# A planned attention-and-expert kernel: one shared stretch of 64-wide products, first sums of values in another bank, constant rows kept, first high parts in place, VectorE charged more in the order

## The chip, the cores and the metric

One core of a Trainium2 chip runs the whole program. TensorE multiplies, VectorE and ScalarE read its banks in PSUM (the accumulator memory, eight banks of 512 float32 columns), GpSimd does little, and SyncE only issues transfers. The metric is the device time of one execution in microseconds. Times of instructions come from one profiled execution.

## What is computed

Decayed causal attention over 8 batches and 8 heads of 576 positions with 64 columns, followed by a gated feed-forward layer over the 4608 positions:

```python
scores = scale * np.matmul(q, k.transpose(0, 1, 3, 2))
cum = np.cumsum(np.log(np.clip(f, 0.0001, 1.0)), axis=-1)
scores = np.where(causal, -1e9, scores + cum[:, :, :, None] - cum[:, :, None, :])
attn = softmax(scores)                       # with 1e-9 added to the sum
x = (attn @ v)                               # heads side by side: 4608 x 512
h = x @ w_in                                 # 512 -> 2048
g = h * np.tanh(log1p(np.exp(h)))
out = g @ w_out                              # 2048 -> 512
```

## The kernel before

The attention is worked in 32 groups (`g`), two heads each, four groups to a batch. `prep(g)` scales a group's q and k and splits each into a high and a low float16 part in the tile `hl`, of which there is one (`NHL = 1`). Transfers carry the parts into two tiles that TensorE reads: `ST1` (three buffers; rows 0 to 63 the high parts of q and k, rows 64 to 69 the cumulative decay in three float16 parts with rows of constants against them, row 70 a maximum) and `ST2` (the low parts). The decay rows of group 0 come straight from `cum3`; those of the other groups, constants included, from `cumd` in device memory, one transfer of seven rows for a group.

Groups 0 to 5 are done in an early form: `max_items` finds row maxima by a first set of scores, `fin` sends them as the row `mr` into row 70, `st_items` makes the scores again with keys in the partitions and `pv_items` multiplies float32 weights with values. Groups 6 to 31 are done in another: `new_st_items` makes scores with queries in the partitions (pieces x, y, z, w), VectorE masks them and takes the minimum, ScalarE the exponent, ScalarE and VectorE split the result, and a transfer transposes it; `new_pv_items` multiplies with the values, head 0 in `one(0)`, head 1 in `one(1)`. The last 64 queries of the two heads share a tile: their scores are piece w (`w_`), with the scores of the last 64 keys (V) in a bank of their own, and their value products are `tail`. Both issue products whose output has 64 partitions, two of which run side by side; `beside` keeps such a stretch together. Products with 128 output partitions stand before and after each stretch.

The feed-forward layer is worked in nine chunks of 512 positions (`m1_items`, `m2_items`). Its weights (`wall`, 32 blocks) are loaded as 64-bit words, converted and split into two float16 parts by VectorE and ScalarE while attention goes on; its products are the 3456 "wall" products of 128x512. The first four groups (one batch) must be through before the first of them.

The order of all this is not written by hand. Every instruction is recorded by `choose` and put out by `emit` (so that nearly all carry one line, L307). `schedule` runs a planner that lists instructions engine by engine: `forward` takes, on each engine, the ready instruction of lowest rank; where an instruction may run on more than one engine (`choose` with several ways) `sooner` compares the ends it plans, with a charge `PEN` for each engine. `floors` keep an instruction from being planned before a time. Where the planner expects TensorE to wait early on, it puts in filler products (`b<-idh`, 128x128) into bank 7 until the first wall product. On the chip each engine takes its list strictly in order and waits at semaphores.

From group 6 on attention's banks are two (0 and 1), taken in turn by `bank`: nine uses for a group. Banks 2 and 3 take the first layer's products, 4 to 7 the second's. SyncE's queue has eight lanes; a transfer waits until the one eight before it has landed.

Of the kernel before, what the change touches and what calls it, by code (L numbers as in the profile page):

```python
# [13 lines left out]
F16 = mybir.dt.float16  # L14
# [51 lines left out]
NGH = 5  # L66
SPD = 0
# [6 lines left out]
PEN = dict(vector=0, scalar=0, gpsimd=4000)  # L74
# [72 lines left out]
class Program:  # L147
# [24 lines left out]
    def choose(self, *ways):  # L172

        r, w, opts = [], [], []
        for way in ways:
            total, port = 0.0, False
            for nth, (eng, method, a, kw) in enumerate(way):
# [5 lines left out]
                if eng == "tensor":  # L183

                    w.append((w[0][0] + "/pe", 0, 1, 0, 1))
# [411 lines left out]
def attn_moe(ctx: ExitStack, tc: tile.TileContext, qk, v, f, w_in, w_out, out):  # L597
# [62 lines left out]
    cumd = dp.tile([7, BH, 2, S], F16, name="cumd")  # L660
# [7 lines left out]

    def decay():
        _, on, cm, r1 = tmp  # L670
        cst = ST1[2][0:BH].rearrange("p j t s -> p (j t) s")
        x = ST1[0]
        nc.vector.memset(x[64:71, :, 0], -1.0)
        nc.gpsimd.memset(x[64:71, :, 1], -MSC)
        nc.gpsimd.memset(x[64:67, :, 1], 1.0)
        for j, c in enumerate((1.0, -1.0, 0.0, -MSC)):
            nc.gpsimd.memset(cst[:, j], c)
        nc.floor = 12500.0
        nc.sync.dma_start(
            out=cumd[0:3, :, 1].rearrange("r h s -> h r s"),  # L680
            in_=cst[:, 0:1].to_broadcast([BH, 3, S]))
        nc.sync.dma_start(
            out=cumd[3:6, :, 0].rearrange("r h s -> h r s"),
            in_=cst[:, 1:2].to_broadcast([BH, 3, S]))
        nc.sync.dma_start(out=cumd[6], in_=cst[:, 2:4])
        nc.floor = 0.0
# [62 lines left out]
    def all_sum(cols, name, least=2.0**-60):  # L749
# [4 lines left out]
        sum_rows(a, m, bank(name))  # L754
# [133 lines left out]
    def amax_v(b):  # L888
# [3 lines left out]
        vam[b] = all_sum(cols, f"va{b}")  # L892
# [30 lines left out]
    st = {g: {} for g in range(B * NP)}  # L923
# [22 lines left out]
    def prep(g):  # L946
# [15 lines left out]
        hl = sp.tile([P, 4, S], F16, name=f"hl{g}", tag="hl", bufs=NHL)  # L962
        for j, (hi, lo) in enumerate(((1, 3), (2, 0))):
# [5 lines left out]
        if g:  # L969
            nc.sync.dma_start(  # L970
                out=ST1[i][64:71].rearrange("r j t s -> r (j t s)"),
                in_=cumd[:, h0 : h0 + 2].rearrange("r j t s -> r (j t s)"))
# [290 lines left out]
    def new_pv_items(g):  # L1263
# [29 lines left out]
        def one(j):  # L1293
# [4 lines left out]
            if j:  # L1298
                tail(o[:, 4])
# [393 lines left out]
```

## Time and profile before

| | us |
|---|---|
| median of 3 runs | 1038.97 (1038.34 to 1054.77) |
| the profiled execution, its own time | 1042.22 |
| its span, first to last instruction | 1040.4 |
| TensorE busy in it | 1005.0 (97%) |
| VectorE busy | 708.0 (68%) |
| ScalarE busy | 671.8 (65%) |

A matmul's busy time in the profile reaches from its issue to its end, 0.38 us for 512 columns, and overlaps the next; what TensorE takes for one is the distance between starts. A busy share near 100% therefore says that it had no gap longer than that overlap. The waits "<-" name what ended an idle time.

### The profile page before, as it was taken

How to read it: one execution, taken by the hardware profiler on the slowest of the kernel's cores; microseconds unless marked ns; L12 is line 12 of the kernel's file. 1: busy time of each engine (PE TensorE's matmuls, PEld its weight loads, DVE VectorE, ACT ScalarE, POOL GpSimd, SP SyncE). 2: the span in 40 equal slices, each digit the busy share in tenths (PEclk: the TensorE clock that was granted, in tenths of full speed). 3: DMA queues.
4: the chain of work that ended last, by engine and by line, in shares of the span. 5: the costliest groups of instructions: out<-in, count | busy, mean ns of one | idle time of the engine just before them, and what ended most of it. 6: DMA issues, size and time to landing. Idle time of an engine off the chain costs nothing.

```text
span 1040.4 us, 20074 instructions
## 1 busy us (share of the span) xinstructions
PE 1005.0 (97%) x7428; PEld 534.3 (51%) x7428; DVE 708.0 (68%) x1972; ACT 671.8 (65%) x1214; POOL 12.8 (1%) x60
## 2 busy tenths in 40 slices
PE   4899999999999999999999999999999999999998
PEld 3788554444545555545455555444555554444443
DVE  7799999988767777677867876778776663121211
ACT  4557898877777887777768786778777672112111
POOL 3000000000000000000000000000000000000000
PEclk9899999999999999999999999999999999999999
DMA  7899967799766876787758766676666432000001
GB/s 210 254 261 242 225 186 190 180 209 194 142 133 138 185 148 139 143 172 145 150 129 163 170 149 137 152 158 121 129 136 132 77 66 65 1 1 31 11 1 41
DMA packets 252805, 143.47 MB, mean 138 GB/s; under 512 B 220349, under 2 KB 221129, under 8 KB 252706
## 3 DMA queue, kind: packets, MB, share of 16 engines
q1 hardware_dynamic: 252706, 142.18, 61.1%
q8 instruction: 58, 0.95, 0.4%
q14 instruction: 41, 0.34, 0.1%
HBM read 48.33 MB, written 12.57 MB: 59 GB/s over the span
## 4 chain that ended last, share of the span: by engine, by line
PE 62%; DVE 17%; ACT 9%; DMA 5%; issue 5%; SPq 1%; ACTq 0%; DVEq 0%
PE b L307 61%; DVE b L307 3%; DVE wall L307 3%; DMA st<-hl 3%; DVE hb L307 2%; ACT st L307 2%; ACT L307 2%; ACT hb L307 2%; DVE hl L307 1%; DVE gl L307 1%; SPq L307 1%; DMA pt<-hb 1%; ACT junk L307 1%; ACT me L307 1%; DVE vv L307 1%
## 5 line engine op out<-in xcount | busy, mean ns | idle before, releaser
L307 PEld LDWEIGHTS <-wall 128*128 128x128 f16 x3456 | 332.1, 98 | 382.1 <-issue 7.6
L307 PE MATMUL b<-xa,wall 128*128 128x512 f16 x1728 | 408.4, 382 | 0.0
L307 PE MATMUL b<-gh,wall 128*128 128x512 f16 x1152 | 360.5, 379 | 0.2
L307 PE MATMUL b<-gl,wall 128*128 128x512 f16 x576 | 218.3, 379 | 0.0
L307 ACT ACTIVATE st<-b,mn 128x512 f32<-128x512 f32 (+1 forms) x260 | 125.6, 525 | 117.8 <-DVE mn L307 86.5
L307 ACT ACTIVATE me<-b,cinv 128x512 f32<-128x512 f32 x144 | 93.2, 685 | 124.2 <-PE b L307 123.5
L307 PE MATMUL b<-st 70*128 70x256 f16 (+14 forms) x948 | 141.4, 287 | 24.1 <-DVE qt L307 14.8
L307 DVE TENSOR_SCALAR gh<-me,gsc 128x512 f16<-128x512 f32 x121 | 57.7, 484 | 140.3 <-ACT me L307 138.6
L307 ACT ACT_TABLE_LOAD x112 | 143.7, 1283 | 9.2 <-DVE mn L307 6.5
L307 DVE TENSOR_TENSOR hb<-st,hb 128x512 f16<-128x512 f32 x156 | 106.8, 689 | 59.6 <-ACT hb L307 59.0
L307 PEld LDWEIGHTS <-st 70*128 70x128 f16 (+5 forms) x948 | 74.2, 103 | 83.7 <-issue 28.6
L307 PE MATMUL b<-vv,pt 128*128 128x65 f16 (+5 forms) x2520 | 114.2, 205 | 2.7 <-ACT st L307 1.4
L307 DVE CUSTOM_DVE_ANT_0 b<-b,mskw 128x512 f32<-128x512 f32 (+1 forms) x208 | 101.7, 501 | 21.5 <-PE b L307 15.0
L307 ACT ACTIVATE hb<-st 128x512 f16<-128x512 f32 x156 | 97.0, 628 | 9.5 <-DMA pt<-hb 8.5
L307 DVE SCALAR_TENSOR_TENSOR gl<-me,gsc,gh 128x512 f16<-128x512 f32 x144 | 103.1, 745 | 0.0
L307 PEld LDWEIGHTS <-pt 128*128 128x128 f16 (+1 forms) x2184 | 65.6, 101 | 17.0 <-issue 5.0
L307 DVE SCALAR_TENSOR_TENSOR hl<-qk,qt,hl 128x576 f16<-128x576 f32 x64 | 50.6, 808 | 0.2 <-ACT hl L307 0.2
L307 ACT ACTIVATE junk<-qk 128x576 bf16<-128x576 f32 x64 | 43.5, 680 | 4.8 <-DMA qk<-in_qk_dram 4.0
L307 DVE SCALAR_TENSOR_TENSOR wall<-wall 128x512 int32<-128x512 int32 x64 | 42.8, 684 | 0.1
L307 PEld LDWEIGHTS b<-vv,pt 128*128 128x128 f32 (+1 forms) x336 | 39.1, 186 | 4.7 <-issue 1.4
L307 DVE DVE_READ_ACCUMULATOR2_ANT mn<- 128x1 f32 x260 | 36.8, 142 | 0.0
L307 ACT ACTIVATE ot<-b,cols 128x512 f32<-128x512 f32 x36 | 24.3, 688 | 16.1 <-PE b L307 11.6
(105 smaller groups left out, 630.8 us busy)
## 6 DMA issues: line engine op xcount, KB each, us to landing
st<-hl SPq DMA_DIRECT2D x192, 144.0 KB
qk<-in_qk_dram SPq DMA_DIRECT2D x32, 576.0 KB
v<-in_v_dram SPq DMA_DIRECT2D x32, 288.0 KB
out_dram<-ot SPq DMA_DIRECT2D x36, 256.0 KB
wall<-in_w_in_dram SPq DMA_DIRECT2D x16, 512.0 KB
wall<-in_w_out_dram SPq DMA_DIRECT2D x16, 512.0 KB
pt<-hb SPq DMA_TRANSPOSE x156
part<-ot SPq DMA_DIRECT2D x8, 256.0 KB
```

The source lines that it names most:

```text
L307: r = getattr(real[eng], method)(*a, **kw)
```

## The change

Five edits. One: from group 10 on, `w_` of group g is no longer an item of its own; `one(1)` of group g-1 calls it, and its 64-wide products and those of `tail` of group g-1 are one `beside` stretch. The scores V take the last 128 columns of the bank that holds `one(1)`'s output, so a group takes eight banks' turns. Two: `all_sum` of the first two batches' values uses bank 7 (`RB`) instead of a turn. Three: `cumd` holds the three decay parts alone; the constants are set once in each `ST1` buffer, and a group's decay comes in two transfers of three rows (`move_cum`). Four: for groups 0 and 1 (`ND = 2`) the high parts for `ST1` are also written straight into it by ScalarE or VectorE, four instructions of 64x576 in place of two transfers. Five: `PEN` of VectorE is 400, and two floors are 12500 (one was 13000, one zero).

```diff
-PEN = dict(vector=0, scalar=0, gpsimd=4000)
+PEN = dict(vector=400, scalar=0, gpsimd=4000)
...
+    def move_cum(x, h):
+        for t, r in enumerate((64, 67)):
+            if h:
+                nc.sync.dma_start(out=x[r : r + 3, :, t], in_=cumd[h : h + 2].rearrange("h r s -> r h s"))
+            else:
+                for j in range(2):
+                    nc.sync.dma_start(out=x[r : r + 3, j, t], in_=cum3[j : j + 1])
...
-        for j in range(2):
-            for t, r in enumerate((64, 67)):
-                nc.sync.dma_start(out=x[r : r + 3, j, t], in_=c[j : j + 1])
-        nc.sync.dma_start(out=cumd[0:3, :, 0].rearrange("r h s -> h r s"), in_=c)
-        nc.sync.dma_start(out=cumd[3:6, :, 1].rearrange("r h s -> h r s"), in_=c)
+        move_cum(ST1[0], 0)
+        nc.sync.dma_start(out=cumd, in_=cum3)
...
-        vam[b] = all_sum(cols, f"va{b}")
+        vam[b] = all_sum(cols, bank(f"va{b}") if b > 1 else psum(RB))
...
+        for j in range(2 * (g < ND)):
+            for h in range(2):
+                r = slice(h * D, (h + 1) * D)
+                nc.choose(*(scaled(ST1[i][0:D, h, j], x[r, j], t[r, j : j + 1], e) for e in SV))
...
-        for j in range(2):
+        for j in range(2 * (g >= ND)):
             nc.sync.dma_start(out=ST1[i][0:D, j], in_=hl[j * D : (j + 1) * D, 1:3])
...
             ps, pv = bank(f"sw_{g}"), bank(f"sv_{g}")
+            if with_tail:
+                st[g - 1]["o1"], pv = pv, pv[:, CH - P : CH]
...
+            if with_tail:
+                every = every[4:] + every[0:4] + st[g - 1]["tail"](st[g - 1]["o1"][:, 4 * (D + 1) : 5 * (D + 1)])
             beside(*every)
...
+            if j and 9 <= g < NG - 1:
+                st[g + 1]["w"]()
+                o = s["o1"]
...
-            a0(lambda: held(13000.0, lambda: load_v(0, VTA)))
+            a0(lambda: held(12500.0, lambda: load_v(0, VTA)))
```

What the planner makes of it stands in the lists of the engines. TensorE's list has the same products, in another order, with 166 fillers where it had 252. Late in the steady part of the program, before the change, one group's tail products (`64x65` into bank 0, two weights of the group's tile `pt`) and the next group's piece w (`64x512` into bank 1, `64x128` into bank 0) stand apart, with expert products around each:

```order
L307 MATMUL b0_0_125<-vv_0_128,pt_6_148 64x65
L307 LDWEIGHTS wall_69
L307 MATMUL b3_0_119<-xa1_87,wall_69 128x512
...
L307 MATMUL b2_0_118<-xa1_87,wall_69 128x512
L307 LDWEIGHTS st1_1_82
...
L307 MATMUL b1_0_116<-st2_1_85 64x512
L307 LDWEIGHTS st1_1_82
L307 MATMUL b0_0_125<-st1_1_82 64x128
...
L307 MATMUL b0_0_125<-st2_1_85 64x128
L307 LDWEIGHTS wall_69
L307 MATMUL b2_0_118<-xa1_87,wall_69 128x512
```

The same place of the change, where bank 0 holds the scores V and the output of `one(1)`:

```order
L309 MATMUL b2_0_118<-xa1_87,wall_69 128x512
L309 LDWEIGHTS st1_0_81
L309 MATMUL b0_0_125<-st1_0_81 64x128
...
L309 MATMUL b0_0_125<-st2_0_84 64x128
L309 LDWEIGHTS st1_0_81
L309 MATMUL b1_0_117<-st1_0_81 64x512
...
L309 MATMUL b1_0_117<-st2_0_84 64x512
L309 LDWEIGHTS pt_3_136
L309 MATMUL b0_0_125<-vv_1_141,pt_3_136 64x65
...
L309 MATMUL b0_0_125<-vv_1_141,tv_1_186 128x65
```

V, w and the tail now follow each other without a 128-wide product between, and the head's other value products come right behind, into the bank that still holds V.

On SyncE near the start, from the first products' rows on, before the change (`st1_0`, `st1_1`, `st1_2` are the buffers of `ST1`; "x4" is four alike):

```order
L307 DMA st2_0_84<-hl_0_109 64x1152 x3
L307 DMA cumd_89<-cum3_90 64x3x576 x2
L307 DMA st2_0_84<-hl_0_109 64x1152
L307 DMA v32_0_110<-in_v_dram 128x576
...
L307 DMA st1_1_82<-cumd_89 7x2304
L307 DMA qk32_0_103<-in_qk_dram 128x1152
L307 DMA st1_1_82<-hl_0_109 64x1152 x2
L307 DMA st2_1_85<-hl_0_109 64x1152 x4
L307 DMA wall_69<-in_w_in_dram 128x1024 x2
L307 DMA st1_2_83<-cumd_89 7x2304
L307 DMA qk32_1_104<-in_qk_dram 128x1152
L307 DMA st1_0_81<-mr_0_127 1x4x128 x2
```

and of the change:

```order
L309 DMA v32_2_112<-in_v_dram 128x576
L309 DMA st1_0_81<-cum3_90 3x1x576 x4
L309 DMA cumd_89<-cum3_90 64x1728
L309 DMA st2_0_84<-hl_0_109 64x1152 x4
L309 DMA v32_3_113<-in_v_dram 128x576
L309 DMA st1_1_82<-cumd_89 3x2x576 x2
L309 DMA qk32_0_103<-in_qk_dram 128x1152
L309 DMA wall_69<-in_w_in_dram 128x1024 x2
L309 DMA st1_2_83<-cumd_89 3x2x576
L309 DMA st1_0_81<-mr_0_127 1x4x128 x2
L309 DMA st1_0_81<-mr_0_127 1x2x64
L309 DMA st2_1_85<-hl_0_109 64x1152 x4
```

Three value loads now stand ahead of the decay rows; the three transfers of constants and those of the high parts of groups 0 and 1 are gone, and group 0's `mr` rows come ahead of group 1's low parts.

On VectorE, where group 1's high parts are made, before the change (`qt_1` is the group's scale, `mx_0` group 0's maxima):

```order
L307 RECIPROCAL qt_1_123<-qt_1_123 128x1
L307 TENSOR_REDUCE mx_0_117<-b2_0_118 128x4
...
L307 TENSOR_REDUCE mx_0_117<-b5_0_121 128x1 x2
L307 TENSOR_SCALAR hl_0_109<-qk32_1_104,qt_1_123 128x576
L307 TENSOR_REDUCE mx_0_117<-b6_0_124 128x2
```

and of the change:

```order
L309 TENSOR_TENSOR mx_0_116<-mx_0_116 128x9
...
L309 RECIPROCAL qt_1_122<-qt_1_122 128x1
L309 TENSOR_SCALAR st1_1_82<-qk32_1_104,qt_1_122 64x576
L309 COPY mr_0_127<-b1_0_117 9x128
L309 TENSOR_SCALAR hl_0_109<-qk32_1_104,qt_1_122 128x576
L309 TENSOR_SCALAR st1_1_82<-qk32_1_104,qt_1_122 64x576 x2
```

Group 0's maxima are finished first, and the casts then go straight into `st1_1`.

## Rows read from the trace of the kernel before

**Rows 1.** The page, busy time of each engine (share of the span), instructions

```profile
PE 1005.0 (97%) x7428; PEld 534.3 (51%) x7428; DVE 708.0 (68%) x1972; ACT 671.8 (65%) x1214; POOL 12.8 (1%) x60
```

**Rows 2.** Windows: length, then PE, PEld, DVE, ACT, POOL busy, PEclk, DMA share, GB/s

```profile
42.00:101.00 59.00, 59.00 (x608) 49.16 (x609) 52.84 (x160) 40.57 (x92) 0.75 (x5) 1.00 0.92 241
101.00:165.00 64.00, 59.56 (x360) 35.27 (x358) 59.57 (x169) 54.40 (x106) 0.28 (x2) 0.95 0.77 204
165.00:240.00 75.00, 71.58 (x522) 35.23 (x521) 69.87 (x214) 61.95 (x115) 0.28 (x2) 0.98 0.88 196
240.00:865.00 625.00, 619.61 (x4868) 316.50 (x4867) 457.41 (x1293) 467.29 (x823) 3.33 (x22) 1.00 0.68 141
```

**Rows 3.** Windows at half clock, the same columns

```profile
153.60:160.40 6.80, 6.80 (x23) 3.28 (x23) 5.54 (x15) 5.79 (x14) 0.14 (x1) 0.50 0.52 146
228.70:232.10 3.40, 3.40 (x10) 1.18 (x8) 2.23 (x9) 2.52 (x7) 0.00 (x0) 0.51 0.59 139
```

**Rows 4.** Timeline of TensorE at the start: start, length, what, count, idle before

```profile
14.83 0.27 PE L307 MATMUL b<-st 70*128 70x128 f16 x1 [14.83 <-DVE qt L307]
...
30.82 0.27 PE L307 MATMUL b<-st 70*128 70x128 f16 x1 [0.28 <-DMA st<-hl]
...
36.27 5.49 PE L304 MATMUL b<-idh 128*128 128x128 f16 x85
41.59 0.53 PE L307 MATMUL b<-st 71*128 71x512 f16 x2
...
45.56 0.39 PE L307 MATMUL b<-vv,pt 128*128 128x65 f32 x2
...
101.23 0.81 PE L307 MATMUL b<-xa,wall 128*128 128x512 f16 x3
```

**Rows 5.** Timeline of SyncE's issues at the start

```profile
9.32 2.95 SPq L307 DMA_DIRECT2D st<-cum  x4
...
23.59 4.71 SPq L307 DMA_DIRECT2D st<-hl  x6
...
34.34 2.09 SPq L307 DMA_DIRECT2D st<-mr  x3
```

**Rows 6.** Timeline of VectorE between 15 and 24 us

```profile
15.02 0.16 DVE L307 RECIPROCAL qt<-qt 128x1 f32<-128x1 f32 x1
15.88 3.35 DVE L307 TENSOR_REDUCE mx<-b 128x4 f32<-128x512 f32 x7 [0.70 <-PE b L307]
...
23.04 0.52 DVE L307 TENSOR_SCALAR hl<-qk,qt 128x576 f16<-128x576 f32 x1 [1.50 <-issue]
```

**Rows 7.** Timeline of TensorE around one tail and one piece w

```profile
513.69 0.25 PE L307 MATMUL b<-vv,tv 128*128 128x65 f16 x3
513.87 0.57 PE L307 MATMUL b<-vv,pt 128*64 128x65 f16 x24
514.37 1.69 PE L307 MATMUL b<-xa,wall 128*128 128x512 f16 x7
...
523.77 0.74 PE L307 MATMUL b<-st 70*64 70x512 f16 x8
524.45 1.90 PE L307 MATMUL b<-xa,wall 128*128 128x512 f16 x8
```

**Rows 8.** Groups by form on VectorE and ScalarE: count, busy us, mean ns, idle before

```profile
L307 DVE TENSOR_SCALAR gh<-me,gsc 128x512 f16<-128x512 f32 x121 | 57.7, 484 | 140.3 <-ACT me L307 138.6
L307 DVE TENSOR_SCALAR hl<-qk,qt 128x576 f16<-128x576 f32 x40 | 20.4, 514 | 15.3 <-DMA st<-hl 11.4 <-issue 3.7
...
L307 ACT ACTIVATE hl<-qk,qt 128x576 f16<-128x576 f32 x24 | 18.3, 772 | 9.3 <-DVE qt L307 6.3 <-DMA st<-hl 2.8
L307 ACT ACTIVATE gh<-me,gsc 128x512 f16<-128x512 f32 x23 | 16.1, 717 | 0.0
```

**Rows 9.** Waits of TensorE between 101 and 240 us: total, times, longest

```profile
PE b L307 <- ACT st L307: 3.2, 4, 1.8
PE b L307 <- ACT pt L307: 2.0, 3, 1.4
```

More of the change, by code (lines that the diff above doesn't have):

```diff
@@ L66 @@
 NGH = 5
+ND = 2
 SPD = 0
@@ L183, in choose @@
                 if eng == "tensor":
-                    w.append((w[0][0] + "/pe", 0, 1, 0, 1))
+                    out = kw["out"] if "out" in kw else a[0]
+                    w.append((out.tensor.name + "/pe", 0, 1, 0, 1))
                 port |= self.shared(eng, method, aps)
@@ L659, in attn_moe @@
     BH = B * H
-    cumd = dp.tile([7, BH, 2, S], F16, name="cumd")
+    cumd = dp.tile([BH, 3, S], F16, name="cumd")
     cum3 = cp.tile([BH, 3, S], F16, name="cum3")
@@ L667, in attn_moe @@
     ft = tmp[0]
+    def move_cum(x, h):
[5 more added lines that the diff above has]
+                    nc.sync.dma_start(out=x[r : r + 3, j, t], in_=cum3[j : j + 1])
     def decay():
         _, on, cm, r1 = tmp
[L671 to L686, printed above, removed]
+        for i, x in enumerate(ST1):
+            (nc.gpsimd if i else nc.vector).memset(x[64:71, :, 0], -1.0)
+            nc.gpsimd.memset(x[64:71, :, 1], -MSC)
+            nc.gpsimd.memset(x[64:67, :, 1], 1.0)
         nc.vector.memset(on, 1.0)
@@ L747, in sum_rows, with all_sum @@
         nc.vector.tensor_copy(out=out, in_=ps)
-    def all_sum(cols, name, least=2.0**-60):
+    def all_sum(cols, ps, least=2.0**-60):
         m = sp.tile([P, 1], F32, name="am_m", tag="am_m", bufs=3)
@@ L753, in all_sum @@
         a = col()
-        sum_rows(a, m, bank(name))
+        sum_rows(a, m, ps)
         return a
@@ L920, in scale_chunk3 @@
             out=cosc[c], in0=cix[c], scalar=1.0 / GSH, in1=top[:, i : i + 1], op0=ALU.mult, op1=ALU.mult)
-    st = {g: {} for g in range(B * NP)}
+    NG = B * NP
+    st = {g: {} for g in range(NG)}
     banks = list(range(NA))
@@ L969, in prep @@
         if g:
-            nc.sync.dma_start(
-                out=ST1[i][64:71].rearrange("r j t s -> r (j t s)"),
-                in_=cumd[:, h0 : h0 + 2].rearrange("r j t s -> r (j t s)"))
-        for j in range(2):
+            move_cum(ST1[i], h0)
+        for j in range(2 * (g >= ND)):
             nc.sync.dma_start(out=ST1[i][0:D, j], in_=hl[j * D : (j + 1) * D, 1:3])
@@ L1168, in new_st_items @@
     def new_st_items(g):
+        with_tail = 9 < g < NG
         i = place1(g)
@@ L1257, in w_ @@
             turn(e, "W")
+        if with_tail:
+            s["w"] = w_
+            return [
+                (begin, 0), (lambda: x_(0), 440), (lambda: y_(0), 440), (z_, 440),
+                (lambda: x_(1), 440), (lambda: y_(1), 440)]
         return [
@@ L1280, in tail @@
         def tail(o):
-            for a in products(o, s["V"], 0, slice(0, P), s["vh"][:, 8], s["vl"][:, 8], True, False):
-                mm(*a)
             every = []
@@ L1288, in tail @@
                     both.append(products(
-                        o[r], s["W"], kt, r, s["vh"][:, 2 * kt + j], s["vl"][:, 2 * kt + j], False, kt == 3))
+                        o[r], s["W"], kt, r, s["vh"][:, 2 * kt + j], s["vl"][:, 2 * kt + j], kt == 0, False))
                 every += [a for x in zip(*both) for a in x]
-            beside(*every)
+            return every
+        s["tail"] = tail
         def one(j):
             n = 4 + j
-            o = bank(f"o{j}_{g}", (P, n, D + 1))
+            if j and 9 <= g < NG - 1:
+                st[g + 1]["w"]()
+                o = s["o1"]
+            else:
+                o = bank(f"o{j}_{g}")
+            o = o[:, 0 : n * (D + 1)].rearrange("p (n d) -> p n d", d=D + 1)
+            if j:
+                if not 9 <= g < NG - 1:
+                    beside(*tail(o[:, 4]))
+                for a in products(
+                        o[:, 4], s["V"], 0, slice(0, P), s["vh"][:, 8], s["vl"][:, 8], False, True):
+                    mm(*a)
             for qt in range(4):
                 blocks(o[:, qt], j, qt)
-            if j:
-                tail(o[:, 4])
             rr = sp.tile([P, 5], F32, name=f"rr{g}_{j}", tag="rr", bufs=4)[:, 0:n]
@@ L1484, in ranked @@
         return g
-    NG = B * NP
     nc.sync.dma_start(out=ft, in_=f)
@@ L1602, in attn_moe @@
             r = KS0 + i * KSS
-            wq.append(ranked([r, 0, 0.1], lambda i=i: convert_weights(i)))
+            wq.append(ranked([r, 0, 0.1], lambda i=i: held(12500.0, lambda: convert_weights(i))))
             wq += [ranked([r + 5, 0, 0.1], lambda k=k: load_weights(k)) for k in behind.get(i, [])]
```

## Prediction

> **What bounds the kernel now.** I read the page's busy times first: TensorE 1005.0 of 1040.4 us, VectorE 68%, ScalarE 65% [rows 1]. So TensorE's own stream sets the time, and a change is worth what it takes out of that stream or out of its gaps. Then the windows, to see where other engines hold it up. Between 240 and 865 us TensorE lacks 625.0 - 619.6 = 5.4 us, and VectorE and ScalarE are busy 73% and 75%: there only TensorE's own stream counts. Between 101 and 240 us it lacks 4.44 + 3.42 = 7.9 us while VectorE is busy 93% in both windows and ScalarE 85% and 83% [rows 2]: here the weights are converted beside attention and all three engines are near their limit. Between 42 and 101 us TensorE is busy throughout (59.0 of 59.0) and VectorE 90% [rows 2]. Before 42 us TensorE mostly waits or runs fillers: its first product is at 14.83, group 1's first at 30.82, the first product of the second scores at 41.59, behind 85 fillers of 5.49 / 85 = 0.065 us, and the first value product at 45.56 [rows 4]. Nothing after 865 us holds attention, so the change has no part there.
>
> **Part one, the shared stretch.** A stretch of 64-wide products costs more than its columns. A 512-column product takes 0.217 us from start to start ((1.90 - 0.38) / 7 for the eight at 524.45, with 0.38 the length of one; the seven at 514.37 give (1.69 - 0.38) / 6 = 0.218), so 65 columns take 0.028 and 128 take 0.054. Tail: three wide products from 513.69 end their slots at 513.77, and the first 64-wide one starts at 513.87: 0.10 us to go in. Its 24 in pairs are 12 x 0.028 = 0.34 us, to 514.21; the next wide one starts at 514.37: 0.16 to come out. Piece w: 523.77 to 524.45 is 0.68 us; its eight in pairs, two of 512 columns and two of 128, are 0.54, so 0.14 to come out, and again some 0.10 to go in [rows 7]. Each stretch thus pays about 0.24 us. One stretch in place of two saves one such payment in groups 10 to 31, 22 times: 22 x 0.24 = **5.3 us**, all of it in TensorE's own stream. The two stretches bound it by 22 x 0.24 and 22 x 0.26, 5.3 and 5.7; what a new wait takes from it is a rival below.
>
> **Part two, the start.** What goes: three transfers of constants on SyncE's queue and, for groups 0 and 1, the transfers of high parts. Those held group 1 up twice. Its scale was ready at 15.02 + 0.16 = 15.2 us, but the cast had to wait for the one tile `hl` (idle 1.50 before 23.04) [rows 6], the transfers were issued from 23.59 [rows 5], and the product came at 30.82 [rows 4]. In the change VectorE first finishes group 0's maxima: two casts more, then reductions from about 16.5 us (15.88 before) for the seven of 3.35 us and two or three more at some 0.5 [rows 6], to about 21.5; eight small instructions at 0.16 to 22.8; then casts at 0.5 into `st1_1`, whose form the trace does not have; the nearest rows are 0.514 for the larger cast on VectorE and 0.772 on ScalarE [rows 8], and I take 0.5. Four make 2.0. Group 1's products then start at about 25 us, 6 earlier. Group 0's `mr` rows are copied at about 23.3; three issues are 2.09 us; the decay rows, issued until 9.32 + 2.95 = 12.27, were in use by 14.83, so such a transfer lands within 2.6 us [rows 4, 5]: 28.0. With group 1's maxima and 41 fillers between, the second scores start at 28 to 31, I take 30: 11.6 us before the old 41.59.
>
> Not all of that stays. The new list has 11 + 8 + 23 + 9 = 51 fillers between those scores and the first value product, where there was none: 51 x 0.065 = 3.3 us. And VectorE, whose list there holds two converted weights, group 2's low parts and group 1's maxima ahead of the values' scale, has some 13 us of work from 26.6 on (25 instructions at 0.15 to 0.2, eleven of about 0.7, two reductions of 0.55): the first value product can start at 38 to 41. I take 39.5, that is 6.0 earlier than 45.56. From there to 101 us TensorE was never idle, so the lead is carried; 35 later fillers against 23 take back 12 x 0.065 = 0.8. Lead at the first wall product: **5.2 us**. Bounds: 10.8 (the scores' lead less 0.8) if VectorE's list is shorter than I think, 2 if the three value loads ahead of the decay rows delay group 0. The two transfers for one in `move_cum` cost 31 more issues of 0.3 to 0.7 us; SyncE is not waited for in the steady part, and at the start the three constants' transfers and four others are gone, so nothing.
>
> **Part three, VectorE's charge.** The lists show up to about 225 us (the seventeenth low part of the gated layer) five casts `gh`, five `hl`, two of the weights and one of x gone from VectorE to ScalarE. At 0.484 and 0.514 [rows 8] and 0.45 for the others that is 2.4 + 2.6 + 1.4 = 6.4 us off VectorE, and at 0.717 and 0.772 [rows 8] 3.6 + 3.9 + 2.1 = 9.6 onto ScalarE. After 240 us both have a quarter of their time free, so the rest of the moves is worth nothing. In 101 to 240 us TensorE loses 7.9 us to gaps, and 6.8 x 0.5 + 3.4 x 0.5 = 5.1 us more to two stretches at 1.2 GHz [rows 3], each behind a gap: 13 in all. A VectorE that is less full and starts earlier takes some of it; but of the gaps 3.2 + 2.0 us end with ScalarE [rows 9], which goes from 116.4 busy us of 139 to 126 (91%). Bounds: minus 10 (nearly all of it) and plus 3 (ScalarE's gaps grow by their half). I take **minus 5**, between them and nearer to the gain, because the earlier conversions also bring the wall products that fill such gaps.
>
> **The clock.** Of the fillers' loss I count nothing. On the rows TensorE fell twice after a wait to a granted clock of 0.50, the 1.2 GHz level, in 153.6 to 160.4 and 228.7 to 232.1 us, and 6.8 us at that level cost 3.4 [rows 3]. The Trainium skill, "TensorE: Matmul & The Clock Gate", section "HAM oscillation — how this bites in real kernels", says that idle gaps drop the clock and that the next products then run at half rate; by it, 86 fillers fewer are 86 chances more to start the second scores slow. One more stretch of the length seen would make the sum 3.4 us worse; that lies in the range.
>
> **Sum.** 5.3 + 5.2 + 5 = 15.5. Against the profiled execution's own time, 1042.2, this gives 1026.7; that execution lay 3.2 above the median of the runs, 1038.97, so for the median **1023.5**.
>
> **Rivals.**
> *The whole lead is kept.* TensorE is full from 42 to 101 us, so if the first values come with the scores the lead there is 10.8, the crowded part gives 9, the stretches 5.3: 25, time 1014. For it: group 1's hold-up disappears entirely. Against it: 51 new fillers say that the planner too sees a gap there. Chance 0.22.
>
> *ScalarE or the loads take it back.* ScalarE at 91% between 101 and 240 us ends TensorE's gaps more often, or the decay rows wait behind 0.86 MB of values so that the start gains nothing. Either leaves the 5.3 of the stretches: about 1034. For it: ScalarE already ends 5.2 of 7.9 us of gaps [rows 9]. Against it: the maxima of group 1 no longer pass through a transfer. Chance 0.27.
>
> *Slower: the shared bank is held.* V's scores sit in the bank that the tail, the three V products and 30 further value products write right behind. If VectorE may read V only after them, w's exponent comes 0.50 (513.87 to 514.37 [rows 7]) + 33 x 0.028 = 1.4 us later, and w's bank and this one come free as much later for the next pieces. With two banks in turn nothing else of attention can go on; only expert products cover it, 15 in the list there, 15 x 0.217 = 3.3 us, against 1.4 us of writing plus about 3 us of reading by VectorE and ScalarE. If the cover fails in full, 22 x 1.4 = 31 us are added: 1054. It decides from 15.5 / 22 = 0.70 us for a group. The Trainium skill, "PSUM — Partial Sum Buffer", section "PSUM bank collisions raise a hardware error", demands that no two engines touch a bank's quadrant at once, which is the reason such an order must hold; no row here shows an overlap. Against it: the whole steady part has only 5.4 us of gaps [rows 2], so cover planned this way mostly holds. Chance 0.05.
>
> **How the numbers follow.** The forecast, 1023.5 with a range of its own from 1018 to 1030, has 0.46; 1014 has 0.22, 1034 0.27, 1054 0.05. Two per cent, about what a measurement of this kernel can tell from no change, is 20.8 us: faster means below 1018.2, slower above 1059.7. Faster: 0.20 from the first rival and 0.05 from the edge of the forecast, 0.25. Slower: 0.02, the far side of the bank. Within 2%: 0.73. The range from 1012 to 1034 holds nearly all of the forecast (0.45), most of the lead's case (0.19) and a good half of the third (0.16): 0.80.
>
> **What would show each step.** Stretches: 26 pairs before; after, 22 stretches of 32 products with one payment of about 0.24 us. Start: group 1's first product near 25 us, second scores near 30, first value product near 39.5, first wall product (101.23 before [rows 4]) near 96. Crowded part: TensorE's gaps in the 139 us behind the first wall product under 5 us, half-clock stretches gone or fewer. Bank: gaps of TensorE in the steady part, 5.4 now, not above 10. The prediction is wrong if the first wall product is not earlier by 2 us, or if those steady gaps more than double.

## The result, and the profile after

The changed kernel took 1030.03 us in the median, against 1042.31 for the kernel before in the same comparison. The ratio is 0.989 with a 95% interval of 0.986 to 0.992: some 11 us faster, inside the 2% band. The profiled execution took 1030.97 us, 11.25 less than the one of before. Executions of one and the same kernel differ by TensorE's mean granted clock (the changed kernel: 1024.79 us at 1.000, 1029.08 at 0.998, 1030.97 at 0.997 and 1042.58 at 0.984), and the ratio leaves out the slow ones (1042.58 here, 1054.77 of the kernel before), which the two medians hold.

The page of the changed kernel, busy time of each engine, answers [rows 1]:

```profile
PE 990.4 (96%) x7342; PEld 527.2 (51%) x7342; DVE 701.7 (68%) x1958; ACT 693.2 (67%) x1236; POOL 17.5 (2%) x62
```

Windows of the changed kernel (columns as in [rows 2]; the first wall product is at 96.43 now):

```profile
38.00:96.40 58.40, 58.24 (x593) 49.00 (x593) 53.23 (x155) 37.02 (x81) 0.46 (x4) 0.97 0.92 235
96.40:165.00 68.60, 64.67 (x407) 38.44 (x404) 67.41 (x205) 65.56 (x131) 0.50 (x2) 1.00 0.72 207
165.00:240.00 75.00, 68.21 (x531) 34.11 (x531) 61.26 (x180) 59.06 (x110) 0.28 (x2) 0.98 0.89 187
240.00:865.00 625.00, 619.26 (x4874) 317.15 (x4873) 458.07 (x1300) 473.14 (x820) 3.05 (x22) 1.00 0.68 140
```

TensorE still lacks 5.7 us of the 625 in the steady part (5.4 before). From 96.4 to 240 us it lacks 3.9 + 6.8 = 10.7, where it lacked 7.9 in [rows 2]; VectorE is busy 98% and ScalarE 96% of the first of these two windows.

To see where the 11 us lie I use one more measure, worked out from the starts of all products: the **time lost** up to a moment is that moment less what the products begun by then take at the full clock (0.216 us for 512 columns, half for those that run in pairs, nothing for fillers). All kernels have the same products, so what is lost is all that differs: gaps, fillers, half clock, and the payments of 64-wide stretches. The level hangs on the price given to the small products (with every column at 0.216/512 us the last line of the table would read 28.7 and 22.7); the differences hardly do.

| time lost, us | before | changed | difference | forecast |
|---|---|---|---|---|
| up to 100 us | 49.1 | 45.5 | -3.6 | -5.2 (lead at the first wall product) |
| 100 to 240 us | 19.3 | 17.9 | -1.4 | -5 |
| 240 to 860 us | 23.7 | 17.7 | -6.0 | -5.3 |

The gain in the second line comes from the clock. From 100 to 240 us half clock cost TensorE 5.1 us before [rows 3] and 1.7 in the changed kernel (210 to 213.5 us), while its gaps grew from 7.9 to 10.7. One execution of each kernel can't say how much of that clock comes from the change.

The start on TensorE in the changed kernel's timeline, against [rows 4]:

```profile
16.29 0.26 PE L309 MATMUL b<-st 70*128 70x128 f16 x1 [16.29 <-DMA st<-cum]
...
26.05 0.31 PE L309 MATMUL b<-st 70*128 70x128 f16 x1
...
31.56 0.53 PE L309 MATMUL b<-st 71*128 71x512 f16 x2
...
40.35 1.86 PE L309 MATMUL b<-vv,pt 128*128 128x65 f32 x15 [0.16 <-DVE cols L309]
...
96.43 1.24 PE L309 MATMUL b<-xa,wall 128*128 128x512 f16 x5
```

Group 1's first product comes at 26.05 (forecast 25), the second scores at 31.56 (30), the first value product at 40.35 (39.5), the first wall product at 96.43 (96). The lead is 10.0 us at the second scores, 5.2 at the first value product and 4.8 at the wall. The very first product is 1.5 us later than before; the part on the start below says why.

One shared stretch in the changed kernel, first on TensorE, then on VectorE (V's minimum is the row with `mskd`, w's the one with `mskw,mn`):

```profile
527.01 0.59 PE L309 MATMUL b<-xa,wall 128*128 128x512 f16 x2
527.53 0.74 PE L309 MATMUL b<-st 70*64 70x128 f16 x8
528.11 0.55 PE L309 MATMUL b<-vv,pt 128*64 128x65 f16 x24
528.59 0.27 PE L309 MATMUL b<-vv,tv 128*128 128x65 f16 x3
528.69 1.08 PE L309 MATMUL b<-vv,pt 128*128 128x65 f16 x30
```

```profile
529.81 0.30 DVE L309 CUSTOM_DVE_ANT_0 b<-b,mskd 128x128 f32<-128x128 f32 x1 [0.83 <-PE b L309]
...
530.20 0.16 DVE L309 TENSOR_SCALAR rr<-b 128x5 f32<-128x5 f32 x1
530.28 0.75 DVE L309 CUSTOM_DVE_ANT_0 b<-b,mskw,mn 128x512 f32<-128x512 f32 x1
```

The two wide products end their slots at 527.01 + 2 x 0.216 = 527.44; the next wide one starts at 528.59. Of these 1.15 us 0.88 are columns by the prediction's prices (0.54 for the scores, 0.34 for the tail), so one payment of 0.27 stands where two stood. And VectorE stands idle for 0.83 us until all products into V's bank are done: it reads V 1.54 us behind the last score product (528.27), and w 2.01 us behind it. In the kernel before a group was read much sooner. There the scores of one group end at 523.77 + 0.74 = 524.51 [rows 7], and VectorE's timeline of before reads:

```profile
525.22 0.29 DVE L307 CUSTOM_DVE_ANT_0 b<-b,mskd 128x128 f32<-128x128 f32 x1
...
525.60 0.76 DVE L307 CUSTOM_DVE_ANT_0 b<-b,mskw,mn 128x512 f32<-128x512 f32 x1
```

That is 0.71 and 1.09 us; over the 23 groups between 240 and 865 us the medians for w are 1.10 before and 2.01 after. The rival's mechanism, a bank held longer by the order of reads behind writes, is there; what it costs is what most of the experiments are about.

### The profile page after: what moved, and what is told of

It reads as the page before. It is cut to its first block, busy times and chain, and to the rows that moved or that the text cites. A ratio compares the mean times of both kernels' runs of the same rounds, so it can differ in the third digit from the quotient of the medians.

```text
span 1029.2 us, 19879 instructions
## 1 busy us (share of the span) xinstructions
PE 990.4 (96%) x7342; PEld 527.2 (51%) x7342; DVE 701.7 (68%) x1958; ACT 693.2 (67%) x1236; POOL 17.5 (2%) x62
## 4 chain that ended last, share of the span: by engine, by line
PE 58%; DVE 17%; ACT 10%; DMA 10%; issue 4%; SPq 1%; POOL 1%; ACTq 0%; DVEq 0%; POOLq 0%
PE b L309 58%; DVE wall L309 4%; ACT L309 3%; DMA qk<-in_qk_dram 3%; DVE hl L309 2%; DMA st<-hl 2%; DMA pt<-hb 2%; DVE b L309 2%; ACT st L309 2%; DVE hb L309 2%; ACT me L309 1%; ACT hb L309 1%; ACT junk L309 1%; DVE gl L309 1%; SPq L309 1%
## 5 line engine op out<-in xcount | busy, mean ns | idle before, releaser
L309 PE MATMUL b<-xa,wall 128*128 128x512 f16 x1728 | 401.6, 379 | 2.9 <-ACT me L309 1.9
L309 ACT ACTIVATE st<-b,mn 128x512 f32<-128x512 f32 (+2 forms) x260 | 125.1, 523 | 69.0 <-DVE mn L309 50.9
L309 PE MATMUL b<-st 70*128 70x128 f16 (+14 forms) x948 | 141.7, 289 | 21.8 <-DMA st<-cum 16.3
L309 DVE TENSOR_SCALAR gh<-me,gsc 128x512 f16<-128x512 f32 x113 | 52.6, 481 | 143.6 <-ACT me L309 142.3
L309 PEld LDWEIGHTS <-st 70*128 70x128 f16 (+4 forms) x948 | 72.6, 104 | 81.9 <-issue 25.7
L309 PEld LDWEIGHTS <-pt 128*128 128x128 f16 (+1 forms) x2184 | 69.9, 102 | 28.5 <-DMA pt<-hb 8.9
L309 ACT ACTIVATE junk<-qk 128x576 bf16<-128x576 f32 x64 | 43.6, 682 | 10.9 <-DMA qk<-in_qk_dram 10.0
L309 ACT ACTIVATE ot<-b,cols 128x512 f32<-128x512 f32 x36 | 24.0, 686 | 20.1 <-PE b L309 10.9
```

Source lines behind the costliest of these rows:

```text
L309: r = getattr(real[eng], method)(*a, **kw)
```

## The experiments

All kernels went through the planner again, so each has an order of its own. The table gathers what the sections read: TensorE's idle time in two windows (length less PE busy), how many of the 22 high parts of values (the cast `vv`) ran on VectorE between 240 and 865 us, and how long behind the last of the score products of w and V VectorE began to read w (median). In old_start and share_only one of the 22 casts lies outside the window.

| run | what differs | ratio to before (95%) | idle 100:240 | idle 240:865 | `vv` on VectorE | w read |
|---|---|---|---|---|---|---|
| before | | 1 | 7.9 | 5.4 | 17 | 1.10 |
| changed | all parts | 0.989 (0.986 to 0.992) | 10.7 | 5.7 | 8 | 2.01 |
| no_share | without the shared stretch | 0.997 (0.995 to 1.000) | 8.0 | 5.3 | 13 | 1.18 |
| charge0 | without the charge | 0.997 (0.995 to 0.999) | 9.5 | 14.7 | 21 | 2.73 |
| old_start | without the new start | 0.992 (0.990 to 0.995) | 6.2 | 7.2 | 8 | 2.01 |
| share_only | before + shared stretch | 1.000 (0.998 to 1.001) | 5.8 | 13.0 | 18 | 2.73 |
| charge_only | before + charge | 0.998 (0.997 to 1.000) | 4.7 | 6.6 | 16 | 1.02 |
| vv_act0 | charge0, `vv` on ScalarE | 0.987 (0.985 to 0.989) | 10.0 | 5.0 | 0 | 2.01 |
| vv_dve | changed, `vv` on VectorE | 1.000 (0.998 to 1.002) | 9.4 | 10.9 | 22 | 2.73 |
| vv_act | changed, `vv` on ScalarE | 0.988 (0.986 to 0.990) | 11.9 | 1.9 | 0 | 2.01 |

**The parts one by one.** First the changed kernel less one part each, and the kernel before with the shared stretch alone.

```diff
-        with_tail = 9 < g < NG
+        with_tail = False
...
-            if j and 9 <= g < NG - 1:
+            if False:
```

> The changed kernel with the shared stretch undone in all groups (w and the tail apart again), the other parts kept. Theory 1, each part pays for itself: 22 groups pay a second entry and exit of 64-wide mode, 22 x 0.215 to 0.25 us = 4.7 to 5.5 us, all of it between 240 and 865 us, so the ratio to the kernel before rises from 0.989 to 0.994. Theory 2, the new plan as a whole made the gain and the stretches are hidden: the ratio stays at 0.989 and TensorE's time lost in 240 to 860 us stays near 17.7. Both: 26 pairs of short stretches (0.77 and 0.60 us) instead of 22 of 1.15.

```diff
-PEN = dict(vector=400, scalar=0, gpsimd=4000)
+PEN = dict(vector=0, scalar=0, gpsimd=4000)
```

> The changed kernel with VectorE charged nothing (the planner's number back at 0), the other two parts kept. Theory 1, as predicted, the charge relieves the crowded part: without it VectorE is the fuller engine from 96 to 240 us, TensorE's gaps there grow from 10.7 by 3 to 5 us, ratio to the kernel before 0.992 to 0.994. Theory 2, the charge only moves work between two engines that are both full from 96 to 165 us (VectorE 98%, ScalarE 96%): the gaps there stay near 10 us, with other releasers, ratio 0.987 to 0.991.

The next one puts back the three transfers of constants, the seven-row transfers of decay, the high parts through `hl`, the turn bank for the first sums of values, and the old floors (the edits two to five of the diff in reverse, but for the charge).

> The changed kernel with the start undone: constant rows written through DRAM as before, group 0's and 1's high parts through their transfers, first values' sums in a turn bank. Theory 1, the lead is carried: group 1's first product near 31 us again, first wall product near 101, time 4.5 to 5.5 us more than the changed kernel, ratio 0.994. Theory 2, from 96 to 165 us ScalarE and VectorE are full and set the pace, so what TensorE brings as lead is lost there: ratio stays at 0.989 to 0.991, and the time lost from 100 to 240 us falls from 17.9 by as much as the start loses.

The kernel before with the shared stretch: its diff is edit one alone.

> The kernel before with the shared stretch alone. Theory 1, each part pays for itself: lost time from 240 to 860 us falls from 23.7 to about 18.5, start and crowded part as before (49 and 19 us lost), 5 us faster, ratio 0.995. Theory 2, the new plan as a whole made the gain: no difference that can be measured, 0.998 to 1.002. A held bank would show as more than 11 us of TensorE gaps from 240 to 865 us.

Measured: without the shared stretch 0.997, and the time lost from 240 to 860 us is 23.6 again (23.7 before, 17.7 changed): theory 1's place, and 5.9 us for the 4.7 to 5.5 it gave; the ratio rose by 0.008 for 0.005, in part by the clock (last section). But the shared stretch alone gives nothing (1.000), and without the charge the changed kernel loses nearly all it had won (0.997). Neither theory of charge0 had that: the time went not in the crowded part (17.6 us lost, 17.9 in the changed kernel) but in the steady one, where TensorE's idle time rose to 14.7 us. Its waits there, in charge0 (total, times, longest):

```profile
PE b L309 <- ACT st L309: 9.9, 15, 1.1
PE b L309 <- DMA pt<-hb: 2.7, 3, 1.2
PE b L309 <- DVE mn L309: 1.2, 2, 0.8
PE b L309 <- DVE x L309: 0.2, 1, 0.2
```

and in the changed kernel:

```profile
PE b L309 <- ACT st L309: 3.6, 8, 0.8
PE b L309 <- DMA pt<-hb: 1.3, 2, 0.8
PE b L309 <- DVE mn L309: 0.4, 1, 0.4
```

"ACT st" is a score product that waits for ScalarE's exponent to leave one of the two banks. Kernels that share the stretch and lack the charge thus idle longer; share_only does too (13.0 us idle, w read at 2.73 us). Whether the late read of w makes these waits is looked at below. The stretches themselves save what they should in all of these: what is lost from 240 to 860 us beyond the idle time is 18.3 us before, and 13.0 in share_only, 13.8 in charge0, 10.8 in old_start, 12.0 in the changed kernel.

Old_start shows what the new start is worth at the end. Its first wall product came at 101.03 us, it had lost 4.8 us more than the changed kernel by 100 us, and 5.7 less from 100 to 240 (12.2 against 17.9): by 240 us nothing of the lead was left, which is theory 2's sign. Its ratio, 0.992, lies between the two theories, and the interval overlaps that of the changed kernel.

The charge alone then:

```diff
-PEN = dict(vector=0, scalar=0, gpsimd=4000)
+PEN = dict(vector=400, scalar=0, gpsimd=4000)
```

> The kernel before with VectorE charged 400 and nothing else. Theory 1, the charge pays only where the shared bank makes VectorE's reading urgent: gaps from 240 to 865 us stay at 5 to 6, lost time there near 23.7, and the crowded part gives 0 to 5 us, ratio 0.995 to 1.000. Theory 2, the charge alone carries most of the gain: ratio 0.990 to 0.993.

It gives 0.998, with 6.6 us idle and 23.6 lost in the steady part: theory 1. Shared stretch and charge are worth nothing or little each, and 0.992 together (old_start, which has both and not the new start).

**Which of the charge's moves it is.** The rows of charge0 between V's and w's minima show what stands there: in most groups the cast `vv`. By form, first charge0, then the changed kernel, from 240 to 865 us (count, busy us, mean ns):

```profile
L309 DVE TENSOR_SCALAR vv<-v,cols 128x576 f16<-128x576 f32 x21 | 16.9, 803 | 0.0
...
L309 ACT ACTIVATE vv<-v,cols 128x576 f16<-128x576 f32 x1 | 0.8, 773 | 0.0
```

```profile
L309 DVE TENSOR_SCALAR vv<-v,cols 128x576 f16<-128x576 f32 x8 | 6.4, 803 | 0.0
...
L309 ACT ACTIVATE vv<-v,cols 128x576 f16<-128x576 f32 x14 | 10.8, 773 | 28.6 <-PE b L309 28.6
```

In charge0 the cast stands ahead of w's minimum in 13 of the 23 groups of the window, in the changed kernel in one. The median of w's read is 2.73 us in the one and 2.01 in the other: 0.72 us, about the cast's 0.80 less the overlap of two instructions. Three kernels force it to one side; the first has no charge.

```diff
-PEN = dict(vector=400, scalar=0, gpsimd=4000)
+PEN = dict(vector=0, scalar=0, gpsimd=4000)
...
-        nc.choose(*(scaled(vh[:, :, 0:D], src, vsc[b], e) for e in (
-            ("scalar", "vector", "gpsimd") if AO & 4 else ("gpsimd",))))
+        nc.choose(*(scaled(vh[:, :, 0:D], src, vsc[b], e) for e in (
+            ("scalar",))))
```

> The changed kernel with VectorE charged nothing, and one choice taken away: the values' high parts (the cast vv, 0.80 us on VectorE) go to ScalarE only. Without the charge 21 of 22 of them ran on VectorE, and w's maximum was read 2.73 us behind its last product, against 2.01 in the changed kernel. Theory 1, that cast standing ahead of w's maximum holds the two banks and makes the gaps: w's maximum back at about 2.0, TensorE's gaps from 240 to 865 us down from 14.7 to 6 to 8, ratio to the kernel before 0.988 to 0.991. Theory 2, the charge helps by moving load in general, or by the luck of the new order: gaps stay at 11 or more, ratio 0.995 to 0.998.

The changed kernel with `("vector",)` in that place:

> The changed kernel, with the charge of 400 kept, but the values' high parts (vv) on VectorE only (8 of 22 ran there). Theory 1, the cast's place ahead of w's maximum is the cause: w's maximum 2.6 to 2.8 us behind its last product, gaps from 240 to 865 us up from 5.7 to 11 to 14, ratio 0.994 to 0.997. Theory 2, the charge's other moves do it: gaps stay at 6 to 8, ratio 0.988 to 0.991.

The changed kernel with `("scalar",)` in that place:

> The changed kernel with the values' high parts on ScalarE only (14 of 22 ran there), charge kept. Theory 1: the last 8 leave VectorE too, gaps from 240 to 865 us 4 to 6, ratio 0.987 to 0.990, at best 2 us faster than the changed kernel. Theory 2: the cast of 0.77 us delays the exponentials on ScalarE as much as it frees VectorE, gaps 8 or more, ratio 0.992 or more.

VectorE in vv_dve, behind a shared stretch whose scores end at 528.89:

```profile
530.82 0.29 DVE L309 CUSTOM_DVE_ANT_0 b<-b,mskd 128x128 f32<-128x128 f32 x1
...
531.21 0.16 DVE L309 TENSOR_SCALAR rr<-b 128x5 f32<-128x5 f32 x1
531.29 0.80 DVE L309 TENSOR_SCALAR vv<-v,cols 128x576 f16<-128x576 f32 x1
532.01 0.75 DVE L309 CUSTOM_DVE_ANT_0 b<-b,mskw,mn 128x512 f32<-128x512 f32 x1
```

and the same place in vv_act0 (scores end at 523.74):

```profile
525.28 0.30 DVE L309 CUSTOM_DVE_ANT_0 b<-b,mskd 128x128 f32<-128x128 f32 x1
...
525.67 0.17 DVE L309 TENSOR_SCALAR rr<-b 128x5 f32<-128x5 f32 x1
525.75 0.75 DVE L309 CUSTOM_DVE_ANT_0 b<-b,mskw,mn 128x512 f32<-128x512 f32 x1
```

The windows from 240 to 865 us, vv_dve and then vv_act0:

```profile
240.00:865.00 625.00, 614.10 (x4847) 314.61 (x4846) 460.57 (x1305) 466.32 (x813) 3.33 (x22) 1.00 0.68 141
```

```profile
240.00:865.00 625.00, 619.96 (x4863) 317.48 (x4860) 452.85 (x1295) 466.66 (x817) 3.05 (x22) 1.00 0.68 140
```

In all three w's read and TensorE's idle time go the way of theory 1, though its sizes were missed: 5.0 us idle for 6 to 8, 10.9 for 11 to 14, 1.9 for 4 to 6. With that one cast on ScalarE the charge isn't needed at all: idle 5.0 us, ratio 0.987, median 1025.31. With it on VectorE the charge doesn't help: idle 10.9 us, and the whole gain is gone (1.000, worse than the 0.994 to 0.997 I had expected; its steady part explains 5 us, and its executions also ran at a lower mean clock, 0.994 against 0.998). vv_act has the shortest idle time of all in the steady part (1.9 us), but loses 3.6 us more than the changed kernel from 100 to 240 us. vv_act0 is the best kernel here; its median is 4.7 us below the changed kernel's, but the intervals of the two ratios overlap.

So it is shown that on which engine this cast runs decides most of the steady part's gain: forced to ScalarE without the charge it brings the gain, forced to VectorE with the charge it takes it away. Over all kernels with a shared stretch the two kinds lie apart, though not by much: with the cast ahead of w in 13 groups TensorE idles 10.9 to 14.7 us (charge0, share_only, vv_dve), and 1.9 to 9.7 where it is ahead in two at most. It is not shown that the held banks are how. Few of the gaps stand where w's bank would make them. In charge0 the 11 groups with w's read at 2.73 us have no gap in the 8 us behind their scores, and of the 14.7 us only 3.5 end with the exponent of w or with the reading of V or w (2.9 of 13.0 in share_only, 0.5 of 10.9 in vv_dve). From one group's scores to the next group's read TensorE idles 0.68 us on average in the 13 groups with the cast ahead, and 0.71 in the ten without. A larger part, 5.3 us in 8 waits, ends with the exponent of another piece that had queued on ScalarE behind a load of its function table; vv_act0 has 2.2 us of these. One such wait in charge0, 12 us behind the read of w, on TensorE, ScalarE and VectorE:

```profile
571.43 0.60 PE L309 MATMUL b<-st 70*128 70x384 f16 x4 [1.10 <-ACT st L309]
```

```profile
567.96 1.27 ACT L309 ACTIVATE me<-b,cinv 128x512 f32<-128x512 f32 x2
569.25 1.28 ACT L309 ACT_TABLE_LOAD   x1
570.54 1.42 ACT L309 ACTIVATE st<-b,mn 128x256 f32<-128x256 f32 x3
```

```profile
565.73 0.14 DVE L309 DVE_READ_ACCUMULATOR2_ANT mn<- 128x1 f32 x1
```

The piece's minimum was there at 565.87, and the exponent began at 570.54. A rival is therefore open: what the cast's engine changes may be the planned order on ScalarE, and with it which exponents come to stand behind a table load. late_set, further below, fits the rival: no cast on VectorE, w read at 2.01 us, 9.7 us idle, 6.6 of it in nine such waits. No run here fixes that order.

**The crowded part.** There I had expected 5 us and found 1.4, and that only through less half clock. TensorE's longest waits from 96 to 240 us in the changed kernel, in place of those of [rows 9]:

```profile
PE b L309 <- DMA pt<-hb: 3.3, 1, 3.3
PE b L309 <- ACT me L309: 1.9, 2, 1.7
PE b L309 <- ACT st L309: 1.4, 4, 0.6
PE b L309 <- DVE gh L309: 1.2, 1, 1.2
```

One wait for a transposing transfer takes 3.3 us, and TensorE then runs at half clock for as long (window 210 to 214 us, mean granted clock 0.58). Another stretch at half clock, from 63 to 66.5 us, follows no such wait: from 38 to 96.4 us TensorE was idle for 0.16 us in all. Two runs leave work out in the crowded part to see which full engine sets the pace. The first takes the weights' scales from a quarter of the columns:

```diff
-        square_sum(wsq[:, step(x, j), x : x + 1], w)
+        square_sum(wsq[:, step(x, j), x : x + 1], w[:, 0:128])
```

> The changed kernel with work left out on ScalarE: the square sums that set the weights' scales run over 128 of 512 columns (32 of them, 0.63 us each, so some 10 us of ScalarE's time less up to 240 us; the scales are then taken from a quarter of the columns). Theory 1, in the crowded part ScalarE (96% busy from 96 to 165 us) sets the pace and eats the lead: time lost from 100 to 240 us falls from 17.9 to 12 or less, total 4 to 6 us faster, ratio 0.983 to 0.985. Theory 2, VectorE (98%) sets it: lost time there stays at 16 to 18, ratio 0.987 to 0.991. Theory 3, single waits for transfers and the half clock behind them set it: no change either.

The second leaves the last three bits out of half of the weights:

```diff
         nc.vector.scalar_tensor_tensor(
-            out=o, in0=r[:, 0::2], scalar=29, in1=o, op0=ALU.logical_shift_right, op1=ALU.bitwise_or)
+            out=o[:, 0:256], in0=r[:, 0:512:2], scalar=29, in1=o[:, 0:256], op0=ALU.logical_shift_right, op1=ALU.bitwise_or)
```

> The changed kernel with work left out on VectorE: the last of three operations of a weight's conversion runs over 256 of 512 columns (32 of them at 0.68 us, some 9 to 10 us of VectorE's time less; half of the weights lack their last three bits). Theory 1, VectorE sets the pace of the crowded part: time lost from 100 to 240 us falls from 17.9 to 12 or less, ratio 0.983 to 0.985. Theory 2, ScalarE sets it: no change there, ratio 0.987 to 0.991. Theory 3, single waits for transfers and the half clock behind them: no change.

Windows of light_act, then light_dve:

```profile
96.00:165.00 69.00, 64.19 (x411) 38.20 (x410) 67.09 (x207) 55.33 (x118) 0.28 (x2) 1.00 0.66 202
```

```profile
96.00:165.00 69.00, 63.82 (x398) 37.60 (x395) 65.14 (x206) 61.76 (x117) 0.57 (x2) 0.95 0.88 239
```

ScalarE's share there fell from 96% to 80%, and TensorE gained little: 16.8 us lost from 100 to 240 us, ratio 0.991 (0.988 to 0.993). So ScalarE's load alone doesn't set the loss. The other run is no clean test: VectorE's busy time from 100 to 240 us stayed where it was (125.8 us, 125.1 in the changed kernel), as other work moved into the freed time; 16.0 us were lost, ratio 0.988 (0.985 to 0.991). VectorE's load, both engines together and theory 3 are left, and none was tested by itself: what makes the single waits stays open.

**The start.** In the changed kernel the decay rows are issued at 12.73 us, against 9.32 [rows 5], and the first product waits for them. VectorE's rows in the changed kernel show a wait for a mask of GpSimd (`msk`) ahead of the running sum (`TENSOR_TENSOR_SCAN`), and casts of the decay that take 1.31 and 1.20 us, while GpSimd sets the constant rows of all three tiles; first VectorE, then GpSimd:

```profile
6.64 0.19 DVE L309 TENSOR_SCALAR mskw<-msk 128x128 bf16<-128x128 f16 x1 [1.26 <-POOL msk L309]
...
6.85 1.39 DVE L309 TENSOR_TENSOR_SCAN st<-st 64x576 f32<-64x576 f32 x1
8.28 1.31 DVE L309 TENSOR_SCALAR cum<-st 64x576 f16<-64x576 f32 x1
...
10.72 1.20 DVE L309 CAST cum<-st 64x576 f16<-64x576 f32 x1
```

```profile
8.22 3.38 POOL L309 MEMSET st<- 7x1152 f16 x3
```

In the kernel before the same sum and casts stand at:

```profile
5.28 1.35 DVE L307 TENSOR_TENSOR_SCAN st<-st 64x576 f32<-64x576 f32 x1 [0.75 <-ACT st L307]
6.67 0.50 DVE L307 TENSOR_SCALAR cum<-st 64x576 f16<-64x576 f32 x1
...
8.01 0.45 DVE L307 CAST cum<-st 64x576 f16<-64x576 f32 x1
```

So 1.6 of the 3.4 us by which the decay rows are late arise ahead of the sum, and 1.56 in the two casts. The next kernel is vv_act0 with six of these settings held back:

```diff
         for i, x in enumerate(ST1):
+            nc.floor = 10500.0 * (i > 0)
             (nc.gpsimd if i else nc.vector).memset(x[64:71, :, 0], -1.0)
...
+        nc.floor = 0.0
```

> The kernel without the charge and with the values' high parts on ScalarE only, in which also GpSimd's setting of the constant rows of the second and third operand tile (six of 1.05 us) is put behind the decay's chain (not before 10.5 us by the planner's clock). Theory 1, those six run beside VectorE's casts of the decay and lengthen them (0.50 and 0.45 us before, 1.31 and 1.20 in the changed kernel): the casts are back at 0.5, the decay rows are issued at about 9.5 us instead of 12.73 (changed kernel) and 11.10 (without the charge), first product near 13.5 to 14.7; of this 0 to 1.5 us reach the end, ratio 0.985 to 0.988. Theory 2, the value loads ahead in the queue delay the decay: issue stays at 11 or later.

The decay rows went out at 10.37 us (11.10 in vv_act0), but not because of the casts: on the chip GpSimd, done with its other work, began the six settings at 5.88 us, and the casts took 1.22 and 0.50, where vv_act0, on which this kernel is built, has 0.96 and 0.45. What went is the wait for the mask: the sum began at 5.63 us, against 6.63 in vv_act0. The first product came at 14.73 (14.65 in vv_act0, and 14.83 in the kernel before). So theory 1 is not settled by this run; that long casts make up part of the changed kernel's delay is read from its rows alone. Theory 2 falls with the queue's rows: in the changed kernel SyncE has nothing to issue between 5.4 and 12.73 us. The time was 0.994 (0.991 to 0.997), worse than vv_act0: 9.7 us idle in the steady part, at 2.01 us for w, in the new order.

**The order alone.**

```diff
-SEED = 122
-NZ = 0
+SEED = 1
+NZ = 2
```

> The changed kernel in a new order only: the planner's ranks get a random addition of up to 2, everything else is the same. What it shows is how far times of one change scatter with the order alone. If the readings by part hold, the time lost from 240 to 860 us stays at 16 to 19 where the values' casts stay on ScalarE (w's maximum at 2.0 us), and the total within 3 us of the changed kernel, ratio 0.986 to 0.992. If the order's luck is as large as the parts, ratio beyond 0.984 or 0.995.

The same change in another order: ratio 0.992 (0.989 to 0.996), at the edge of what I had expected. Time lost from 240 to 860 us is 18.0 (17.7), w is read at 2.01 us, so the steady part's number held in this order (in late_set it did not); from 100 to 240 us it loses 12.6, against 17.9. Its executions range from 1025.55 us at a mean clock of 1.000 to 1039.34 at 0.988.

## Why the prediction was right, and where it was not

The forecast was 1023.5 with 1012 to 1034; it came to 1030.03, within 2% as most of the chance said. By its steps:

- **Stretches, 5.3 us: right in size.** 22 stretches of 32 products, each with one payment of 0.27 us; a pair took 0.767 + 0.596 = 1.363 us before and 1.148 now, so 22 x 0.215 = 4.7 us. The Trainium skill, "TensorEngine Tiling (Array Packing)", section "Key Properties", says that a change of tiling mode drains TensorE; the trace agrees, and shows that the price is nearly all that of the change (0.23 us for 8 products, 0.26 for 24, 0.27 for 32, at the prediction's prices for columns), not of the products.
- **Start, 5.2 us: right at the wall product (4.8), too large further on.** All four moments came within 1.6 us of the forecast ones. That the loads of values would delay group 0 was the wrong reason for a delay that did come (1.5 us): VectorE waited for GpSimd's mask, and its casts took longer. What failed is that the lead at the wall counts to the end: over all kernels here the new start has lost 44.3 us by 100 us (mean of ten) and the old one 50.5 (mean of four); by 240 us it is 61.8 and 65.7, but the two that differ in the new start alone stand at 63.4 (changed) and 62.5 (old_start). Some 4 us or nothing remain; the runs don't settle it.
- **Crowded part, 5 us: the mis-sized term, and its mechanism failed.** It gave 1.4 in this order. TensorE's gaps behind the first wall product were to fall from 7.9 to under 5 us, and they rose to 10.7; what got shorter is half clock, from 5.1 us lost to 1.7. The kernels here lose between 12.2 and 21.5 us from 100 to 240 us, with the charge and without it, so a term of 5 us was smaller than what a new order alone moves (17.9 to 12.6 in jit0). I took TensorE's gaps for a quantity that less work on another engine shrinks; with ScalarE's work cut the loss was still 16.8.
- **The charge after 240 us, nothing: wrong, and the largest error.** "After 240 us both have a quarter of their time free, so the rest of the moves is worth nothing." The load hardly moved (both engines are busy 72% to 76% of the steady part in charge0 and in the changed kernel), but on which engine one cast runs did matter: with the shared stretch, the charge takes TensorE's idle time from 14.7 to 5.7 us, and the move of `vv` alone takes it to 5.0. How the cast makes the gaps stays open.
- **The rival of the held bank: the late read is real, its cost is not shown.** The forecast of 1.4 us more for the exponent of w is 0.9 in the changed kernel and 1.6 without the charge. The trace agrees with the rule on banks that the prediction names: VectorE reads V's bank only when the last product into it is done, after an idle 0.83 us in the row shown. By the sign that the prediction set (gaps of the steady part above 10 us) the rival comes true in share_only and charge0, where (14.7 - 5.4) / 22 = 0.42 us for a group is more than the 0.215 saved, and share_only ends at 1.000; but only 3.5 of those 14.7 us stand at V or w. It did not reach the 0.70 from which the kernel would have become slower than before with all parts in.

So the sum was too large by the crowded part's 3.6 us and the start's 1.6, and too small by 0.7 in the steady part. That the total came out so near is in part luck: the crowded part gained by the clock while its gaps grew, and that the stretches' gain came out at all hung on the charge, of which I had counted nothing there.

## What to carry to other kernels

A bank, or any buffer taken in turn, is held from its first write to its last read, so ask of a shared buffer which instruction stands ahead of the last read on the reading engine; then look whether the gaps stand there. Here one cast of 0.8 us on an engine that was 73% busy went with more idle time than the change saved, yet most of that idle time stood elsewhere. Before a planner's cost is tuned, look for the one instruction whose engine matters and fix that one; in vv_act0 it did all of the charge's work in the steady part. And where an order is planned anew, terms of a few microseconds in a part where all engines are near full are below the scatter of the order itself.

## What the runs showed of the hardware that was not expected

VectorE's casts were longer beside GpSimd instructions that only set memory: 64x576 casts of 0.50 and 0.45 us took 1.31 and 1.20 beside settings of about 1.1 us each (3.38 for three). The Trainium skill, "SBUF — State Buffer", section "Who interferes with whom", has it that VectorE's casts can, in some of their modes, use a pair of ports that it shares with GpSimd, and that whichever is second then waits for the whole instruction of the other. Casts longer by 0.81 and 0.75 us, less than one setting, agree with it; the cast that stayed at 0.50 in late_set while settings were going on is not explained by the rows.

TensorE's mean granted clock differs between executions of one kernel, and the time with it: for jit0 from 1.000 to 0.988 the time rises by 13.8 us, and over 28 executions of the kernel before a fitted line gives some 8 us for 0.01. A part of each ratio here is this clock (0.998 in the mean for the changed kernel, 0.994 for the kernel before and for no_share), and one profile says little about it. By that line, an estimate, some 3 of the changed kernel's 11 us are clock and some 8 are left; jit0, the same change at a mean clock of 0.993 like the kernel before in the same comparison (0.994), is 8 us faster.
